# Placing global keys and queries a batch ahead in short GpSimd copies, with the k and q casts moved into the attention

## The chip, the core and the metric

The kernel runs on one core of one Trainium2 chip. The metric is the device time of one execution in microseconds (us): it covers everything from the first to the last instruction and the little that lies around them. Before the change three runs took 376.73, 377.93 and 377.97 us, a median of 377.93 us.

The core's engines work side by side and only wait for one another through semaphores. PE is the matrix engine, ACT the activation engine, DVE the vector engine, POOL (GpSimd) the general engine, and SP an engine that here only issues DMAs. GpSimd issues DMAs as well, and it executes its list strictly in order: a copy that stands behind a DMA that has to wait, waits too.

## What is computed

Windowed attention with eight global positions, followed by a two-layer block with a sine activation. All inputs are float32.

```python
batch, n_heads, seq, head_dim = (8, 8, 576, 64)
window = 32
scores = scale * np.matmul(q, k.transpose(0, 1, 3, 2))
mask = np.abs(pos[:, None] - pos[None, :]) <= window
mask = mask | is_global[:, None] | is_global[None, :]
scores = np.where(mask, scores, -1000000000.0)
attn = softmax(scores)
x = np.matmul(attn, v)          # heads side by side: 4608 tokens x 512
h = x @ w_in                    # 512 -> 2048
s = np.sin(alpha * h)
g = h + s * s / (alpha + 1e-09)
out = g @ w_out                 # 2048 -> 512
```

(The softmax is written out in the reference; the eight entries of `global_idx` mark the global positions.)

## The kernel before

The work goes batch by batch, b = 0 to 7. For each batch there is an attention (`phase_a`, `attention`) over four pairs of heads, and then a GEMM with w_in (`gemm1`) over sixteen groups of 128 hidden units. The second GEMM, with w_out (L1041), is cut into single matmuls that `fill` drops between the other work, so that PE has something to do. The kernel's order is written out by hand; each engine takes its own instructions in the order in which the program names them.

**Operands of the attention.** A batch's keys lie in `KX` and its queries in `QX`, two buffers each, taken in turn by `b % 2`. `KX` has, for each pair of heads and each of twelve tiles of 48 tokens, 128 columns; 8 of every 64 are the global keys. `QX` has four columns for global queries in each of seven places of a row. The values lie in `VX`, likewise with two buffers.

**How a batch's operands arrive.**
- `cast_qk(b)` (L324, DMAs at L329): GpSimd issues two DMAs of 576 KB each, k first and then q, which turn float32 into bf16 in a DRAM buffer of the pool `dramp` (two buffers for each of the two).
- `turn_qk(b)` (L334, L338): SP issues two transposing DMAs from there into the tiles `kt` and `qt`.
- `place(b, ...)` (L343, copies at L348 and L355): DVE copies from `kt` and `qt` into `KX` and `QX`. From batch 3 on the eight copies for batch b are spread over the attention of batch b - 1; two of them come at its very end (`beside(NHP)`, L880). For batch 3, in the attention of batch 2, four of them do.
- `place_globals(b)` (L365): GpSimd copies the global keys from `kTg` (two copies of 64 partitions by 384 elements, L369) and the global queries from `qTg` (two of 128 by 112, L374) into the other columns of `KX` and `QX`.
- `load_v(b, hps)` (L386, DMAs at L391): GpSimd issues four DMAs for each pair of heads. They overwrite the buffer that batch b - 2 used, so each group of four waits until PE has finished that pair's products (L781). `load_vg(b)` (L396) does the same for the global values from SP. A DMA of GpSimd's also waits for the landing of the DMA eight places earlier in its list, whose semaphore it shares.

**Inside an attention,** for each pair of heads: scores on PE (L739), exp on ACT (L747), the mask on DVE (L750), the two products with the values and with ones on PE (L781), the inverse of the sums on ACT (L807, L810), sums for the global positions (L791) and the normalising product (L813) on DVE. The products of the next pair of heads need the PSUM bank that L813 reads. Beside this, DVE squares the previous batch's x for a later check (L915, L920, L923). After the last pair come the reciprocal and two small products for the global rows (L823, L827).

**Inside gemm1,** for each group of 128 hidden units: eight matmuls on PE (L982), sine on ACT (L1014), its square on ACT (L1018) or DVE (L1020), and the sum into `H2` on DVE (L1022), which frees the PSUM bank. Three banks go round, so the fourth group waits for the first group's L1022.

**The main loop** decides the order on GpSimd. For batches 1 to 5 it issues, ahead of `gemm1(b)`, the casts for batch b + 2, the first pair's V loads, the placing for batch b + 1, and then the other V loads. For batch 0 the placing of batch 1 stands inside `gemm1`, for batch 6 that of batch 7 stands alone:

```python
        if 0 < b and b + 2 < B:
            cast_qk(b + 2)
            load_v(b + 2, (0,))

            place_globals(b + 1)
            load_v(b + 2, range(1, NHP))
            load_vg(b + 2)
        elif 0 < b < B - 1:
            place_globals(b + 1)
        gemm1(b)
```

The attention of batch b stands in the program before iteration b, and GpSimd runs ahead until the V loads make it wait for that attention's products. So the placing for batch b + 1 is executed in the midst of the attention of batch b.

Of the kernel before, what the change touches and what calls it, by code (L numbers as in the profile page):

```python
# [18 lines left out]
NG = 8  # L19
KT = 48  # L20
# [227 lines left out]
def kernel(  # L248
# [11 lines left out]
    nc = tc.nc  # L260
    B, H, S, D = q.shape
# [3 lines left out]
    NT12 = S // KT  # L265
    NHP = H // 2
# [27 lines left out]
    KX = [main.tile([P, NHP, NT12, P], DT.bfloat16, name=f"KX{i}") for i in range(2)]  # L294
# [9 lines left out]
    kTg = main.tile([P, NHP, NG, B], DT.bfloat16, name="kTg")  # L304
# [19 lines left out]
    def cast_qk(b):  # L324

        cast[b] = []
        for src, name in ((k, "kd"), (q, "qd")):
            t = dramp.tile([P, H * S * D // P], DT.bfloat16, name=name)
            nc.gpsimd.dma_start(  # L329
                out=t[:], in_=src[b].rearrange("h s d -> (h s d)").rearrange("(p f) -> p f", p=P)  # L330
            )
            cast[b].insert(0, t)

    def turn_qk(b):  # L334

        turned[b] = [trp.tile([P, H * HALF], DT.bfloat16, name=name) for name in ("qt", "kt")]
        for i in (1, 0):
            nc.sync.dma_start_transpose(  # L338
                out=turned[b][i][:], in_=cast[b][i][:].rearrange("p (r c) -> (p r) c", c=P)
            )  # L340
        del cast[b]
# [22 lines left out]

    def place_globals(b):  # L365

        for t in range(2):
            rows = slice(t * D, (t + 1) * D)
            nc.gpsimd.tensor_copy(  # L369
                out=KX[b % 2][rows, :, :, t * D + KT : t * D + KT + NG],  # L370
                in_=kTg[rows, :, None, :, b].to_broadcast([D, NHP, NT12, NG]),
            )
        for y in range(2):
            nc.gpsimd.tensor_copy(  # L374
                out=globals_of(b, slice(0, P), y),
                in_=qTg[:, :, None, y::2, b].to_broadcast([P, NHP, 7, 4]),
            )

    def globals_of(b, rows, y):

        q0 = QX[b % 2][rows, :, y, PAD : PAD + 4]
        return bass.AP(
            tensor=q0.tensor, offset=q0.offset, ap=[list(q0.ap[0]), [2 * QROW, NHP], [SEG, 7], [1, 4]]
        )

    def load_v(b, hps=range(NHP)):  # L386
        for hp in hps:
            for t in range(2):
                for y in range(2):
                    r = t * D + y * 24  # L390
                    nc.gpsimd.dma_start(  # L391
                        out=VX[b % 2][r : r + 24, hp, :, t * D : t * D + D],
                        in_=v[b, 2 * hp + t].rearrange("(i a y) d -> y a i d", a=24, y=2)[y],
                    )

    def load_vg(b):  # L396
        for h in range(H):
            t = h % 2
            src = VGb[b::B, h * D : (h + 1) * D] if b else VG0[h::H]
            nc.sync.dma_start(  # L400
                out=VX[b % 2][t * D + KT : t * D + KT + NG, h // 2, :, t * D : t * D + D],
                in_=src[:, None, :].to_broadcast([NG, NT12, D]),
            )
# [35 lines left out]
    for half in range(2):  # L439
        for w, src in ((1, k), (0, q)):  # L440
            nc.gpsimd.dma_start(
                out=nat[w][D * half : D * half + HK],
                in_=src[0, HH * half : HH * half + HH].rearrange("h (i r) d -> (h i) (r d)", r=KT),
# [22 lines left out]
    for t in (gidx8, gp64):  # L466
        nc.vector.memset(t[:].bitcast(DT.int32), 0)
    nc.sync.dma_start(
        out=g64[:],
        in_=bass.AP(tensor=global_idx.tensor, offset=global_idx.offset, ap=[[1, NG], [0, B], [1, 1]]),  # L470
# [3 lines left out]
    for t in (0, D):  # L474
        nc.sync.dma_start(out=gp64[t + KT : t + KT + NG], in_=global_idx[:, None])
        nc.sync.dma_start(
            out=gidx8[t + KT : t + KT + NG],
            in_=bass.AP(tensor=global_idx.tensor, offset=global_idx.offset, ap=[[0, NG], [1, NG]]),
# [29 lines left out]
    for i, bits in enumerate((B - 1, D - 1)):  # L508
        nc.vector.tensor_scalar(
            out=rowi[:, i : i + 1], in0=prow[:], scalar1=bits, scalar2=None, op0=ALU.bitwise_and  # L510
# [6 lines left out]
        out=cond[:, 0:1], in0=pm, scalar1=float(NH), scalar2=float(1 - KT), op0=ALU.is_ge, op1=ALU.mult  # L517
# [3 lines left out]
        out=kpos[:], in0=pm, scalar=2.0, in1=cond[:, 0:1], op0=ALU.mult, op1=ALU.add  # L521
    )
    nc.vector.scalar_tensor_tensor(
        out=kpos[:], in0=cond[:, 1:2], scalar=float(4095 + KT), in1=kpos[:], op0=ALU.mult, op1=ALU.add
# [4 lines left out]
        out=rowf[0 : NG * B, 4:5], in0=rowf[0 : NG * B, 0:1], scalar=float(S), in1=rowf[0 : NG * B, 3:4], op0=ALU.mult, op1=ALU.add  # L529
# [19 lines left out]
    for name, src in (("k", k), ("q", q), ("v", v)):  # L549
        g0[name] = VG0 if name == "v" else setup.tile([NG * B, D], DT.bfloat16, name="g0" + name)  # L550
        nc.gpsimd.indirect_dma_start(
            out=g0[name][:], out_offset=None, in_=src[0].rearrange("h s d -> (h s) d"),
# [16 lines left out]
        out=band[:], in0=qrel[:], scalar1=float(WIN * WIN) + 0.5, scalar2=None, op0=ALU.is_le  # L569
    )  # L570
    for t in (0, D):
# [4 lines left out]
        out=M2, in_=band[:].rearrange("p e x c -> p e (x c)")[:, None].to_broadcast([P, 6, 2, WCOL])  # L576
# [49 lines left out]
    def place_global_queries(t, copy):  # L626
# [15 lines left out]
        out=first[:], in0=gf[:], scalar1=gpf[:, 0:1], scalar2=None, op0=ALU.not_equal  # L642
# [3 lines left out]
        out=later[:], in0=jrow[:], scalar1=pm, scalar2=float(-KT), op0=ALU.subtract, op1=ALU.is_ge  # L646
# [5 lines left out]
        out=cond[:, 2:3], in0=pm, scalar=float(KT + NG - 1), in1=cond[:, 1:2], op0=ALU.is_le, op1=ALU.mult  # L652
# [5 lines left out]
        out=far[:], in0=qpos[:], scalar1=float(WIN * WIN) + 0.5,  # L658
# [13 lines left out]
    for w, name in ((1, "k"), (0, "q")):  # L672
        pg[w] = both[0:D, 32 + w * 64 : 64 + w * 64].bitcast(DT.bfloat16)
        nc.tensor.transpose(
            out=pg[w][:], in_=g0[name][:], identity=identb[0 : NG * B, 0 : NG * B]
# [283 lines left out]
    def gemm1(b):  # L959
# [28 lines left out]
        for nt in range(NT):  # L988
# [9 lines left out]
            if b == 0 and nt == 11:  # L998

                load_w_out()  # L1000
                cast_globals_v()
                place_globals(1)
                load_v(1, (2, 3))
                load_vg(1)
# [94 lines left out]
    def phase_a(b_att, b_moe):  # L1099
        def beside(at):  # L1100

            if b_moe is None:
                if at == -1:
                    nc.vector.tensor_scalar(out=recipT[:], in0=alphaT[:], scalar1=1e-9, scalar2=None, op0=ALU.add)
                    nc.vector.reciprocal(out=recipT[:], in_=recipT[:])
                if at == 0:
                    second_half()
                    nc.gpsimd.memset(VX[1][:].bitcast(DT.int32), 0)
                    nc.gpsimd.memset(QX[1][:].bitcast(DT.int32), 0)
                    nc.gpsimd.memset(KX[1][:].bitcast(DT.int32), 0)  # L1110
                    turn_qk(1)
                    nc.gpsimd.tensor_copy(out=seen[:], in_=turned[1][1][0:1, 0:1])
                    load_w_in((2, 3))
                    load_v(1, (0, 1))
                    gather(v, gv)
                return
            if at == 0:
                if b_moe == 2:
                    column_norms(zn[:, 0, :])
                if b_moe >= 3:  # L1120
                    token_norms(b_moe - 3, zn[:, 1, :])
            if 0 <= at < 2 and b_moe:
                square_x(b_moe, at)
            if b_att == 1 and at == 0:
                place_rest(1)
                place_rest(0)
            for which, t, y in places_at(b_att, at):
                place(b_att + 1, which, t, y, nc.vector.tensor_copy)
            if b_moe == 0 and at == 2:
                turn_qk(2)  # L1130
            if b_moe == 1 and at in (2, 3):
                square_w(at)

        if b_moe is not None:
            waiting.append(gemm2(b_moe))
        attention(b_att, beside)

    phase_a(0, None)
    for b in range(B):
        if 0 < b and b + 2 < B:  # L1140
            cast_qk(b + 2)
            load_v(b + 2, (0,))

            place_globals(b + 1)
            load_v(b + 2, range(1, NHP))
            load_vg(b + 2)
        elif 0 < b < B - 1:
            place_globals(b + 1)
        gemm1(b)
        if b + 1 < B:  # L1150
            if b == 0:
                cast_qk(2)
                load_v(2)
                load_vg(2)
            elif b + 2 < B:
                turn_qk(b + 2)
            phase_a(b + 1, b)
# [45 lines left out]
```

## Time and profile before

| what | value |
|---|---|
| median of three runs | 377.93 us (376.73 to 377.97) |
| the profiled execution | 376.68 us, of which its span is 375.0 us |
| mean granted PE clock | 0.991 |
| first scores of batches 2, 3, 4, 5, 6, 7 | 97.99, 140.69, 181.25, 221.32, 261.59, 300.78 us |
| GpSimd's copies L369 | 14, mean 1018 ns; shortest 862 ns |
| GpSimd's copies L374 | 14, mean 463 ns; shortest 371 ns |
| DVE's L1022, 576 wide | 805 to 817 ns |
| casts, from issue to landing (median) | k 6.4 us, q 8.9 us |

The profile is that of one execution. Times on the left of a timeline are microseconds from the start of the span, followed by the length, the engine, the line of the program, the operation and its tiles; `x4` joins four equal instructions that follow one another. In square brackets stands the time that the engine was idle before, and what ended it. Two operations in a row are read with care: a record can begin while the one before it is still finishing, so it is the length beside a like instruction elsewhere that tells of a delay.

### The profile page before, as it was taken

The page shows a single profiled execution, that of the slowest core. Times are in us where ns is not written, and L with a number is a line of the kernel's source. Part 1 is how long each engine was busy: PE and PEld are TensorE (multiplying, and loading weights), DVE is VectorE, ACT ScalarE, POOL GpSimd, SP SyncE. Part 2 cuts the span into 40 slices and gives each one's busy share as a digit, 9 for nine tenths or more (in the row PEclk, how much of TensorE's full clock was granted, in tenths as well). Part 3 has the DMA queues.
Part 4 walks back from the last instruction along what each step waited for, and adds up shares of the span by engine and source line. Part 5 has one row for each costly group of instructions (what it writes and reads, how often), then busy time and mean ns, then how long its engine had stood idle before and what let it go on. Part 6 is the DMA issues. An engine that isn't in the chain of part 4 may idle for free. (4 is left out here: it accounts for less than half of the span.)

```text
span 375.0 us, 8335 instructions
## 1 busy us (share of the span) xinstructions
PE 337.6 (90%) x2994; PEld 228.9 (61%) x3040; DVE 287.8 (77%) x624; ACT 294.1 (78%) x566; POOL 132.1 (35%) x204
## 2 busy tenths in 40 slices
PE   1578979998998899999989999999999999999992
PEld 1467646765566666667657766667676766665441
DVE  5776997589789887988888888888788876789400
ACT  7789997899889788788978897879888788875110
POOL 7993695578277001840087005740000000000001
PEclk9999999999999999999999999999999999999998
DMA  7999999999988863799159934636221001000221
GB/s 118 115 174 192 152 166 179 160 208 163 207 164 75 138 110 78 91 104 216 31 60 105 187 69 69 64 52 111 74 50 38 0 30 59 29 2 28 75 68 49
DMA packets 103578, 38.06 MB, mean 102 GB/s; under 512 B 94138, under 2 KB 98250, under 8 KB 103082
## 3 DMA queue, kind: packets, MB, share of 16 engines
q0 software_dynamic: 56640, 18.56, 42.7%
q1 hardware_dynamic: 46890, 18.89, 23.9%
q8 instruction: 26, 0.43, 0.5%
q14 instruction: 22, 0.18, 0.1%
HBM read 37.15 MB, written 17.83 MB: 147 GB/s over the span
## 5 line engine op out<-in xcount | busy, mean ns | idle before, releaser
L1041 PE MATMUL zo<-w_out,H 128*128 128x512 bf16 x530 | 143.3, 379 | 1.9
L982 PEld LDWEIGHTS <-w_in 128*128 128x128 bf16 x1024 | 98.6, 98 | 48.0 <-issue 12.6
L391 POOL DMA_DIRECT2D VX<-in_v_dram x128 | 83.1, 658 | 106.8 <-PE zd L781 90.4
L1041 PEld LDWEIGHTS <-H 128*128 128x128 bf16 x576 | 52.2, 97 | 37.9 <-issue 0.3
L747 ACT ACTIVATE E<-ring 128x480 bf16<-128x480 f32 x96 | 54.3, 568 | 25.5 <-PE ring L739 24.8
L750 DVE TENSOR_TENSOR E<-E,MASK 128x480 bf16<-128x480 bf16 x96 | 36.5, 410 | 16.7 <-ACT E L747 15.6
L1022 DVE SCALAR_TENSOR_TENSOR H<-s,recipT,zn 128x576 bf16<-128x576 bf16 x47 | 38.2, 814 | 8.4 <-ACT s L1018 5.0
L1018 ACT ACTIVATE s<-sb 128x576 bf16<-128x576 bf16 (+1 forms) x62 | 42.7, 689 | 2.0
L1069 POOL DMA_INDIRECT out_dram<-osb,grow x1 | 1.0, 1003 | 122.6 <-SPq L1171 122.6
L739 PE MATMUL ring<-QX,KX 128*128 128x120 bf16 x384 | 38.2, 226 | 6.5 <-ACT E L747 3.0
L739 PEld LDWEIGHTS <-KX 128*128 128x128 bf16 x384 | 29.1, 102 | 22.6 <-issue 11.0
L1014 ACT ACTIVATE sb<-zn,alphaT 128x576 bf16<-128x576 f32 (+1 forms) x47 | 34.8, 740 | 9.7 <-PE zn L982 9.7
L1022 DVE SCALAR_TENSOR_TENSOR H<-s,recipT,zd 128x576 bf16<-128x576 bf16 x39 | 31.7, 814 | 6.6 <-ACT s L1018 4.7
L1020 DVE TENSOR_TENSOR s<-sb 128x576 bf16<-128x576 bf16 (+1 forms) x66 | 31.1, 472 | 5.7 <-ACT sb L1014 5.4
L1047 ACT COPY osb<-zo 128x512 f32<-128x512 f32 x36 | 20.8, 578 | 18.4 <-PE zo L1041 18.4
L1022 DVE SCALAR_TENSOR_TENSOR H<-s,recipT,zr 128x576 bf16<-128x576 bf16 x39 | 31.7, 812 | 3.9 <-ACT s L1018 1.9
L1014 ACT ACTIVATE sb<-zd,alphaT 128x576 bf16<-128x576 f32 (+1 forms) x39 | 28.9, 741 | 6.9 <-PE zd L982 5.4
L781 PEld LDWEIGHTS <-VX 128*128 128x128 bf16 x448 | 26.0, 98 | 12.5 <-issue 6.8
L1014 ACT ACTIVATE sb<-zr,alphaT 128x576 bf16<-128x576 f32 (+1 forms) x39 | 28.9, 741 | 4.4 <-PE zr L982 4.4
L982 PE MATMUL zn<-xlast,w_in 128*128 128x288 bf16 (+1 forms) x192 | 28.8, 289 | 1.2 <-DVE H L1022 0.7
L781 PE MATMUL zn<-E,VX 128*128 128x120 bf16 (+2 forms) x336 | 26.3, 209 | 3.7 <-DVE xlast L813 2.2
L982 PE MATMUL zn<-xT,w_in 128*128 128x288 bf16 x184 | 26.9, 286 | 3.0 <-DVE H L1022 1.9
(161 smaller groups left out, 489.8 us busy)
## 6 DMA issues: line engine op xcount, KB each, us to landing
VX<-in_v_dram POOLq DMA_DIRECT2D x128, 36.0 KB, 3.9
kd<-in_k_dram POOLq DMA_DIRECT2D x7, 576.0 KB, 6.4
qd<-in_q_dram POOLq DMA_DIRECT2D x7, 576.0 KB, 8.9
w_in<-in_moe_w_in_dram POOLq DMA_DIRECT2D x4, 512.0 KB, 5.7
w_out<-in_moe_w_out_dram POOLq DMA_DIRECT2D x4, 512.0 KB, 8.9
out_dram<-osb SPq DMA_DIRECT2D x8, 256.0 KB
out_dram<-osb SPq DMA_DIRECT2D x8, 224.0 KB
out_dram<-osb SPq DMA_DIRECT2D x8, 192.0 KB
```

Of the source, the lines that this page charges most:

```text
L391: nc.gpsimd.dma_start(out=VX[b % 2][r : r + 24, hp, :, t * D : t * D + D], in_=v[b, 2 * hp + t].rearrange("(i a y) d -> y a i d", a=24, y= ...
L739: nc.tensor.matmul(out=ps[:, e * WCOL : (e + 1) * WCOL], lhsT=kx[:, hp, i, :], rhs=qx[:, hp, :, s0 : s0 + 60], start=True, stop=True, skip ...
L747: nc.scalar.activation(out=Eg, in_=ps[:, 0 : 4 * WCOL], func=AF.Exp, scale=scale, accum_out=EA[:, n : n + 1])
L750: nc.vector.tensor_tensor(out=Eg, in0=Eg, in1=MASK[:, 4 * g : 4 * g + 4, :].rearrange("p i c -> p (i c)"), op=ALU.mult,)
L781: nc.tensor.matmul(out=out_t[:, half, :, a - half * CUT : z - half * CUT], lhsT=OB[:] if key else VXb[:, hp, i, :], rhs=E[:, i, :, a - s0 ...
L982: nc.tensor.matmul(out=h[e][:, 0:W], lhsT=lhsT, rhs=xT[:, c, e, 0:W], start=(c == 0), stop=(c == CT - 1), skip_group_check=True,)
L1014: nc.scalar.activation(out=sb[:, es, 0:W], in_=h[:, :, 0:W], func=AF.Sin, scale=alphaT[:, nt : nt + 1])
L1018: nc.scalar.activation(out=s2[:, :, 0:W], in_=sb[:, :, 0:W], func=AF.Square)
L1020: nc.vector.tensor_tensor(out=s2[:, :, 0:W], in0=sb[:, :, 0:W], in1=sb[:, :, 0:W], op=ALU.mult)
L1022: nc.vector.scalar_tensor_tensor(out=H2[:, nt, r0 : r0 + S].rearrange("p (e c) -> p e c", e=2)[:, es], in0=s2[:, es, 0:HALF], scalar=recip ...
L1041: nc.tensor.matmul(out=ops[:], lhsT=H2[:, nt, blk * P : (blk + 1) * P], rhs=w_out[:, nt, :], start=(nt == 0), stop=(nt == NT - 1),)
L1047: nc.scalar.copy(out=osb[:], in_=ops[:])
```

## The change

`place_globals` copies the global keys for one pair of heads at a time: eight copies of 64 by 96 elements in place of two of 64 by 384. The two copies of the queries stay.

In the main loop the placing for batch b + 2 is issued in iteration b, behind the V loads of the first three pairs of heads; before, it was that of b + 1, behind the first pair's. Iteration 1 keeps the placing of batch 2 where it was and adds that of batch 3. Iteration 6 places nothing any more. The casts for batches 5, 6 and 7 are issued in iterations 2, 3 and 4, between the V loads of the first and the second pair; before, they opened iterations 3, 4 and 5. The casts for batches 3 and 4 stay at the head of iterations 1 and 2.

```diff
     def place_globals(b):
 
-        for t in range(2):
-            rows = slice(t * D, (t + 1) * D)
-            nc.gpsimd.tensor_copy(
-                out=KX[b % 2][rows, :, :, t * D + KT : t * D + KT + NG],
-                in_=kTg[rows, :, None, :, b].to_broadcast([D, NHP, NT12, NG]),
-            )
+        for hp in range(NHP):
+            for t in range(2):
+                rows = slice(t * D, (t + 1) * D)
+                nc.gpsimd.tensor_copy(
+                    out=KX[b % 2][rows, hp, :, t * D + KT : t * D + KT + NG],
+                    in_=kTg[rows, hp, None, :, b].to_broadcast([D, NT12, NG]),
+                )
...
         if 0 < b and b + 2 < B:
-            cast_qk(b + 2)
+            if b < 3:
+                cast_qk(b + 2)
             load_v(b + 2, (0,))
-
-            place_globals(b + 1)
-            load_v(b + 2, range(1, NHP))
+            if b == 1:
+                place_globals(2)
+            elif b + 3 < B:
+                cast_qk(b + 3)
+            load_v(b + 2, (1, 2))
+            place_globals(b + 2)
+            load_v(b + 2, (3,))
             load_vg(b + 2)
-        elif 0 < b < B - 1:
-            place_globals(b + 1)
         gemm1(b)
```

In the built program PE, DVE, ACT and SP have the same instructions in the same order as before, each waiting for the same engines; only GpSimd's list differs. The lines after `place_globals` move down by one.

## The prediction, made before the changed kernel had run

> **What bounds the kernel now.** I read the busy shares first, then PE's waits in order of time, then DVE and GpSimd at the same moments. The chain that ended last covers under 1% of the span (it is the tail's last scatter), so it is no guide here.
>
> ```profile
> PE 337.6 (90%) x2994; PEld 228.9 (61%) x3040; DVE 287.8 (77%) x624; ACT 294.1 (78%) x566; POOL 132.1 (35%) x204
> ```
>
> PE sets the time, so only a moment in which PE stands idle can be won. In the attentions of batches 3, 4 and 5 there is exactly one such moment each. PE's timeline:
>
> ```profile
> 156.16 0.36 PE L781 MATMUL zn<-E,VX 128*128 128x88 bf16 x4 [0.84 <-DVE xlast L813]
> ...
> 196.63 0.36 PE L781 MATMUL zn<-E,VX 128*128 128x88 bf16 x4 [1.03 <-DVE xT L813]
> ...
> 236.76 0.36 PE L781 MATMUL zn<-E,VX 128*128 128x88 bf16 x4 [0.84 <-DVE xlast L813]
> ```
>
> PE waits 0.84, 1.03 and 0.84 us for the normalising product L813. DVE at that place in batch 4 (with copies of GpSimd beside it) and in batch 6 (without any):
>
> ```profile
> 191.04 1.95 DVE L920 TENSOR_TENSOR SQ<-SQ 128x1152 bf16<-128x1152 bf16 x2
> 193.03 0.89 DVE L923 TENSOR_TENSOR SR<-SQ 128x288 bf16<-128x288 bf16 x1
> 193.93 0.57 DVE L355 COPY KX<-kt 64x1152 bf16<-64x1152 bf16 x1
> 194.54 1.11 DVE L750 TENSOR_TENSOR E<-E,MASK 128x480 bf16<-128x480 bf16 x3
> ```
>
> ```profile
> 271.37 1.24 DVE L920 TENSOR_TENSOR SQ<-SQ 128x1152 bf16<-128x1152 bf16 x2
> 272.65 0.31 DVE L923 TENSOR_TENSOR SR<-SQ 128x288 bf16<-128x288 bf16 x1
> 272.97 0.45 DVE L355 COPY KX<-kt 64x1152 bf16<-64x1152 bf16 x1
> 273.46 1.05 DVE L750 TENSOR_TENSOR E<-E,MASK 128x480 bf16<-128x480 bf16 x3
> ```
>
> The same work is 0.71 + 0.58 + 0.12 + 0.06 = 1.47 us longer in batch 4. GpSimd then:
>
> ```profile
> 191.31 2.44 POOL L369 COPY KX<-kTg 64x384 bf16<-64x384 bf16 x2
> 193.81 0.93 POOL L374 COPY QX<-qTg 128x112 bf16<-128x112 bf16 x2
> 194.69 2.60 POOL L391 DMA_DIRECT2D VX<-in_v_dram  x4
> 198.35 2.54 POOL L391 DMA_DIRECT2D VX<-in_v_dram  x4 [1.07 <-PE zd L781]
> ```
>
> So these four copies of place_globals and DVE's bf16 work hold each other up; in batch 6, where the kernel places nothing, PE has no such gap. L1022, with one operand in PSUM, keeps 807 to 817 ns in all 125 of its 576-wide runs, copies beside it or not: it is not touched.
>
> **What the removal is worth.** Measure from the first scores of an attention to the fourth w_in group of the GEMM behind it: 140.69 to 165.08 = 24.39 us in batch 3, 24.16 in batch 4, 24.36 in batch 5, and 23.27 (261.59 to 284.86) in batch 6. From there to the next first scores it is 15.91 in batches 4 and 5 and 15.92 in batch 6, so the difference is kept: 1.12 + 0.89 + 1.09 = 3.10 us for the three. The lower bound is the three gaps alone less the 0.25 us that batch 6 waits at its fourth group, 2.71 - 0.75 = 1.96. In batch 2 placing (107.92 to 111.09) also ran beside DVE, but there ACT runs without a pause from 109.05 to 119.8 and sets the end of the attention: gain 0.
>
> **Where the copies go.** PE, DVE, ACT and SP keep their streams, and the engines they wait for. GpSimd alone is reordered: for batches 4 to 7 the placing now stands behind the third of four groups of V loads, which waits for the products of head pair 2, so it falls on the end of the attention. The eight KX copies have 96 elements. Alone a 384-element copy takes 0.87 us and a 112-element one 0.37, so 1.8 ns per element and 0.34 us for 96; the placing grows from 1.77 + 0.69 = 2.5 to some 3.4 us. GpSimd is 35% busy and nobody waits for these columns until a whole batch later, so the length itself costs nothing.
>
> What is late next is DVE's chain into the GEMM, here in batch 6:
>
> ```profile
> 282.15 0.32 DVE L827 TENSOR_TENSOR xlast<-GS,RG 128x16 bf16<-128x16 f32 x2
> 282.48 0.92 DVE L348 COPY QX<-qt 64x1152 bf16<-64x1152 bf16 x2
> 283.43 0.46 DVE L1020 TENSOR_TENSOR s<-sb 128x576 bf16<-128x576 bf16 x1
> 284.00 0.81 DVE L1022 SCALAR_TENSOR_TENSOR H<-s,recipT,zn 128x576 bf16<-128x576 bf16 x1
> ```
>
> It ends at 284.81 and PE's fourth group starts at 284.86: no cover, every hit counts. In batch 6's frame L827 is at +20.56 and L1020 ends at +22.3. The third V group can start at +15.9, but its fourth DMA must wait for the DMA eight places earlier. That wait is seen once today, behind casts:
>
> ```profile
> 67.94 0.64 POOL L391 DMA_DIRECT2D VX<-in_v_dram  x1 [1.01 <-DMA kd<-in_k_dram]
> 70.83 0.64 POOL L391 DMA_DIRECT2D VX<-in_v_dram  x1 [2.26 <-DMA qd<-in_q_dram]
> ```
>
> In the new order the cast of q stands eight places before it. It would be issued at +10.6 (V loads from +7.44, 2.63 us, then 0.53 for k) and takes 8.9 to land (the page's median), +19.5; behind that DMA stand the ten copies and the last V group; the copies run from about +20.1 to +23.5. They meet L827 twice, L348 twice and L1020: 5 hits in batches 3 and 4. In batch 5 no cast stands there, copies run from +18.5, four pieces are left by +20.56: 4 hits. In batch 2 L348 has four copies (121.06, 1.99 us); pieces are left for 5 hits. Together 19.
>
> Price of a hit: the 112-element copies cost L355 0.12 (0.57 against 0.45), L750 0.06 to 0.07 (three times) and 0.2 (twice, 110.25: 1.43 for three), L1020 0.18 (0.63 against 0.45): mean 0.125, a third of 0.37. A 384-element copy costs 0.39 (L1020, 0.84) to 0.58 (L923), about 0.52 of its 0.87. So 0.25 to 0.35 of a copy is hidden, and a piece of 0.34 costs 0 to 0.09; I take 0.05, the cut of the same instruction being the nearest row. Eight pieces at 0.05 and two at 0.125: 0.065 a hit, bounds 0.025 and 0.097. Cost 19 x 0.065 = 1.24 (0.5 to 1.8).
>
> **The early batches.** place_globals(3) moves into the GEMM of batch 1, 92 to 95.5: five hits of 0.065 on L355 and L348 there, 0.33, of which about 0.2 is cover (PE's last group starts at 95.93, its L1022 ends at 95.69): 0.13, up to 0.3. The shorter pieces of place_globals(2) replace L1020's 0.84 and 0.63 in front of PE's gap of 0.59 at 85.75: -0.3 (0 to -0.4). place_globals(1) likewise shortens L348's pair of 1.25 at 50.44: -0.2 (0 to -0.4).
>
> **The casts.** They fly in the attention, not under the GEMM. Issuing costs GpSimd 0.53 each, as before. V loads queued behind them land some 9 us later, for use 30 us on. Cast 6 today overlaps the transposes of batch 5 (5.37 us to issue at 169.11, against 2.67 at 134.56); that ends, and nobody waited. Outputs on SP share the engines with the casts; no PE or ACT wait in these stages names a DMA, and the three osb buffers cover it. I count 0; without that cover ACT's L1047 would be late.
>
> **Sum.** -3.10 + 1.24 + 0.13 - 0.3 - 0.2 = -2.2 us. The profiled execution took 376.68 (span 375.0 and 1.7 around it), so 374.5; its time lies 1.25 under the median of 377.93, where the same step gives 375.7, my forecast. With all bounds together: -3.4 (-3.10 + 0.5 + 0 - 0.4 - 0.4) to +0.2 (-1.96 + 1.84 + 0.3).
>
> **Rivals.** (1) *The hits cost as much as they did.* One price decides: with h per hit the sum is -3.6 + 19h + (5h - 0.2), level at 0.16. At 0.125, as the 112-element rows, it is -0.8: 377.1, no change to be told. For it: eight of ten pieces are almost that length. Against: the proportion above.
>
> (2) *Slower: each operation waits out a whole piece.* At h = 0.34 the sum is -3.8 + 24 x 0.34 = +4.4: 382.3. Place: L827 to L1020 behind each attention. For it: L923's 0.58 was more than half of a long copy, and a queue of ten pieces always has one ready. Against: no row shows a whole copy lost. The Trainium skill, "SBUF — State Buffer", section "SBUF: two separate sides", says this of the port pair that GpSimd shares with VectorE: whichever starts first holds it "for the whole instruction" and the other blocks fully. By that rule splitting a copy does not divide the lock, it deals it out to more operations, and rival 2 follows; the rows agree that L1022 is spared and that an operation blocks, but a hit of 0.12 beside a copy of 0.37 is less than the whole.
>
> (3) *Casts land early*, the third V group isn't held, and the copies end beside L813: two hits each, 8 x 0.065 = 0.5, the sum -3.4: 374.5.
>
> That the change misses its aim, because PE's gaps have another cause, is refuted well by batch 6; I give it no case.
>
> **How the numbers follow.** Forecast 0.60, rival 1 0.14, rival 2 0.16, rival 3 0.10. Half a per cent, about what a measurement of this kernel tells from no change, is 1.9 us. Of the forecast's 0.60 I put 0.42 beyond it and 0.18 within. Faster 0.42 + 0.10 = 0.52, same 0.18 + 0.14 = 0.32, slower 0.16. The forecast's own range is 374.5 to 378.1 on the median; since the profiled execution lies lower I start at 373.6, and reach to 379.0 towards rival 2.
>
> **What would show it.** PE's waits for L813 at the second product of batches 3 to 5 gone, L920 and L923 there back at 1.24 and 0.31; GpSimd's copies beside L827 to L1020, L348's pair at 1.0 to 1.1 and L1020 at 0.5; PE's fourth group waiting 0.3 to 0.6 for L1022; first scores to fourth group at 23.5 to 23.7. Wrong if L1020 or L348 grow by 0.3 each, if the placing takes over 5 us, or if PE or ACT waits for a DMA.

## The result and the profile after

The changed kernel takes 373.98 us (median of 12 executions, 372.53 to 376.25) beside 377.34 us for the kernel before on the same chip (12 executions, 376.09 to 380.35). The ratio is 0.9911, with a 95% interval of 0.9884 to 0.9938: 3.4 us faster. A second measurement of the same kernel, with other runs beside it, gave 373.06 us and 0.990 (0.9872 to 0.9929). Ratios leave disturbed executions out, so for a kernel whose executions scatter the median and the ratio need not agree.

The profiled execution took 373.89 us, its span is 372.2 us. In code behind `place_globals` the line numbers are one higher than before: L813 is now L814, L1022 is L1023. The busy shares come first:

```profile
PE 336.6 (90%) x2994; PEld 228.8 (61%) x3040; DVE 282.8 (76%) x624; ACT 293.5 (79%) x566; POOL 140.2 (38%) x246
```

DVE is 5.0 us less busy with the same 624 instructions, and GpSimd 8.1 us more with 42 more. PE's timeline at the second product of batches 3, 4 and 5, where it stood 0.84, 1.03 and 0.84 us for L813:

```profile
156.10 0.36 PE L782 MATMUL zn<-E,VX 128*128 128x88 bf16 x4
...
195.36 0.36 PE L782 MATMUL zn<-E,VX 128*128 128x88 bf16 x4
...
234.69 0.36 PE L782 MATMUL zn<-E,VX 128*128 128x88 bf16 x4
```

No bracket stands behind them: the three gaps are gone. DVE just ahead of that place in batch 4:

```profile
190.97 1.24 DVE L921 TENSOR_TENSOR SQ<-SQ 128x1152 bf16<-128x1152 bf16 x2
192.24 0.31 DVE L924 TENSOR_TENSOR SR<-SQ 128x288 bf16<-128x288 bf16 x1
192.56 0.45 DVE L355 COPY KX<-kt 64x1152 bf16<-64x1152 bf16 x1
193.05 1.04 DVE L751 TENSOR_TENSOR E<-E,MASK 128x480 bf16<-128x480 bf16 x3
```

All four are back at the lengths that batch 6 had before. GpSimd's timeline in the same batch shows where the copies went, and what held them:

```profile
200.71 0.64 POOL L392 DMA_DIRECT2D VX<-in_v_dram  x1 [1.71 <-DMA qd<-in_q_dram]
201.34 3.49 POOL L370 COPY KX<-kTg 64x96 bf16<-64x96 bf16 x8
204.89 0.98 POOL L375 COPY QX<-qTg 128x112 bf16<-128x112 bf16 x2
```

And DVE beside them, with PE's fourth w_in group behind:

```profile
201.41 0.47 DVE L828 TENSOR_TENSOR xlast<-GS,RG 128x16 bf16<-128x16 f32 x2
201.90 1.04 DVE L348 COPY QX<-qt 64x1152 bf16<-64x1152 bf16 x2
202.97 0.49 DVE L1021 TENSOR_TENSOR s<-sb 128x576 bf16<-128x576 bf16 x1
203.56 0.81 DVE L1023 SCALAR_TENSOR_TENSOR H<-s,recipT,zn 128x576 bf16<-128x576 bf16 x1
```

```profile
203.18 1.03 PE L1042 MATMUL zo<-w_out,H 128*128 128x512 bf16 x4
204.43 1.14 PE L983 MATMUL zn<-xT,w_in 128*128 128x288 bf16 x8 [0.23 <-DVE H L1023]
```

PE runs five matmuls of w_out there; the first has no record in this profile, only its weight load has. Against the same instructions in batch 6 of before (0.32, 0.92, 0.46) the new collisions lengthen DVE's chain by 0.15 + 0.12 + 0.03 = 0.30 us, and PE now stands 0.23 us for the last of it.

The profiled span is 2.77 us shorter (374.96 to 372.19), and the stages say where: the first scores of batch 0 come 0.36 earlier; batches 0 and 1 together take 1.06 more; the stage of batch 2 (first scores to fourth w_in group) takes 0.25 more; those of batches 3, 4 and 5 take 1.01, 0.91 and 1.01 less; what follows the fourth group of batch 7 takes 0.59 less; the rest, a few hundredths at a time, makes 0.20.

### The profile page after: what moved, and what is told of

Its sections match the earlier page's. It is cut to its first block, busy times and chain, and to the rows that moved or that the text cites. A ratio compares the mean times of both kernels' runs of the same rounds, so it can differ in the third digit from the quotient of the medians.

```text
span 372.2 us, 8377 instructions
## 1 busy us (share of the span) xinstructions
PE 336.6 (90%) x2994; PEld 228.8 (61%) x3040; DVE 282.8 (76%) x624; ACT 293.5 (79%) x566; POOL 140.2 (38%) x246
## 5 line engine op out<-in xcount | busy, mean ns | idle before, releaser
L1023 DVE SCALAR_TENSOR_TENSOR H<-s,recipT,zn 128x576 bf16<-128x576 bf16 x47 | 38.2, 814 | 9.0 <-ACT s L1019 5.6
L1023 DVE SCALAR_TENSOR_TENSOR H<-s,recipT,zd 128x576 bf16<-128x576 bf16 x39 | 31.7, 814 | 6.5 <-ACT s L1019 4.6
L1021 DVE TENSOR_TENSOR s<-sb 128x576 bf16<-128x576 bf16 (+1 forms) x66 | 30.5, 463 | 6.2 <-ACT sb L1015 5.9
L1048 ACT COPY osb<-zo 128x512 f32<-128x512 f32 x36 | 20.8, 576 | 18.3 <-PE zo L1042 18.2
L1023 DVE SCALAR_TENSOR_TENSOR H<-s,recipT,zr 128x576 bf16<-128x576 bf16 x39 | 31.7, 813 | 4.2 <-ACT s L1019 2.1
```

Source lines behind the costliest of these rows:

```text
L1021: nc.vector.tensor_tensor(out=s2[:, :, 0:W], in0=sb[:, :, 0:W], in1=sb[:, :, 0:W], op=ALU.mult)
L1023: nc.vector.scalar_tensor_tensor(out=H2[:, nt, r0 : r0 + S].rearrange("p (e c) -> p e c", e=2)[:, es], in0=s2[:, es, 0:HALF], scalar=recip ...
L1048: nc.scalar.copy(out=osb[:], in_=ops[:])
```

## The experiments

Every kernel was run beside the kernel before. The stages are those of the one profiled execution, in us; medians and ratios are over all executions of that measurement.

| kernel | batch 2 | batch 3 | batch 4 | batch 5 | median us (before) | ratio (95%) |
|---|---|---|---|---|---|---|
| before | 26.52 | 24.39 | 24.16 | 24.36 | 377.34 | 1 |
| after | 26.77 | 23.38 | 23.25 | 23.35 | 373.98 (377.34) | 0.9911 (0.9884–0.9938) |
| after, again | 26.61 | 23.47 | 23.25 | 23.36 | 373.06 (376.41) | 0.990 (0.9872–0.9929) |
| nothing placed from batch 3 on | 26.46 | 23.38 | 22.97 | 23.35 | 373.24 (376.41) | 0.9916 (0.9895–0.9937) |
| before, short copies | 29.25 | 23.62 | 23.19 | 23.59 | 373.82 (376.08) | 0.9941 (0.992–0.9962) |
| before, placed later | 26.93 | 23.33 | 23.06 | 23.55 | 376.05 (376.08) | 0.9966 (0.9934–0.9999) |
| before, casts moved | 27.33 | 24.88 | 24.64 | 24.35 | 378.45 (376.08) | 1.0072 (1.0046–1.0099) |
| after, long copies | 27.91 | 24.88 | 24.82 | 23.35 | 385.56 (376.08) | none |
| after, casts back | 26.63 | 23.39 | 23.14 | 30.08 | 380.76 (376.41) | 1.0105 (1.0031–1.018) |
| the same, batch 1 long | 26.63 | 23.37 | 23.11 | 30.27 | 380.49 (376.41) | 1.013 (1.0076–1.0184) |
| casts back, all transposes sooner | 39.03 | 23.39 | 23.11 | 23.38 | 385.49 (376.57) | 1.0216 (1.0187–1.0245) |
| placed later, all transposes sooner | 39.61 | 23.34 | 23.06 | 23.35 | 387.29 (376.57) | 1.0243 (1.0187–1.0298) |
| casts back, one transpose pair sooner | 26.63 | 23.37 | 23.10 | 23.36 | 373.71 (376.38) | 0.9929 (0.9904–0.9954) |
| after, batch 1 long | 26.59 | 23.53 | 23.18 | 23.39 | 373.51 (376.57) | 0.9914 (0.9894–0.9934) |

### What the copies cost: none placed, and the kernel after again

```diff
             load_v(b + 2, (0,))
-            place_globals(b + 1)
+            if b == 1:
+                place_globals(2)
             load_v(b + 2, range(1, NHP))
             load_vg(b + 2)
-        elif 0 < b < B - 1:
-            place_globals(b + 1)
```

> The kernel before without the placing for batches 3 to 7 (their global keys and queries stay those of batches 1 and 2, so that part of the attention is left out of the computation); batches 1 and 2 are placed as before, casts as before. It is the bound for any place and length of the copies. Theory P: stages of batches 3 to 5 at 23.27 as batch 6, time 2.5 to 4 us below before; after is within 0.7 us of it, that is, the new collisions cost next to nothing. Rival (a cause other than the copies holds L813 up in batches 3 to 5): stages 24 and more.

> The kernel after once more, so that the next three stand beside it on one chip. Stages 23.4, 23.25 and 23.35 in batches 3 to 5 as in its first profile. Time 2 to 4 us below before. First scores of batch 1 at 53.7 if the w_in load lands early in this execution (PE's wait for it 0.2 us), at 54.9 if late (1.9).

Without any placing the stages of batches 3 to 5 lose 1.01 + 1.19 + 1.01 = 3.21 us, and the time is 0.9916 of before. So the copies are the cause, and the kernel after (0.9911 and 0.990) stands at this bound. Batch 4 falls below the 23.27 that theory P named: with no copies at all PE has no wait at its fourth group,

```profile
202.22 1.24 PE L1041 MATMUL zo<-w_out,H 128*128 128x512 bf16 x5
203.41 1.14 PE L982 MATMUL zn<-xT,w_in 128*128 128x288 bf16 x8
```

where batch 6 of before waits 0.25. Against this bound the new collisions of the kernel after cost 0.00, 0.28 and 0.00 us in batches 3, 4 and 5, and 0.09, 0.28 and 0.01 in its second run. The other theory (stages of 24 and more) is out. The second run of after gave its stages again; its first scores of batch 1 came at 54.31, with 1.3 us of waiting for w_in, between the two cases that were named.

### One part of the change at a time

Short copies in the old place and order (the change to `place_globals` alone):

> The kernel before, with the eight short copies at the old places and nothing moved. Stage = first scores to fourth w_in group, 24.39, 24.16 and 24.36 us in batches 3, 4 and 5 before, 23.38, 23.25 and 23.35 after. Theory P (the shared work of DVE and GpSimd: the gain is that the placing no longer lies in front of L813): the ten pieces still stand there, at 0.03 to 0.13 a hit for some six hits, 0.2 to 0.8 of the 1.47 us of DVE delay is left, so PE's gap mostly closes too: stages 23.4 to 23.9, time 1 to 2.5 us below before. Rival L (only the length of the pieces matters, the place doesn't): stages as after, 23.3. Rival C (the casts' flight is what was in the way): stages unchanged at 24.2 to 24.4, time as before. In the start of batch 1 the longer placing makes PE's wait for its first scores longer by up to 1.4 us by all of them.

Long copies, placed behind the third V group, casts as before (the main loop's change without the casts):

> The kernel before, with only the place of the placing moved: behind the third pair's V loads and a batch ahead, in the two long copies; casts at their old place. Theory P: DVE in front of L813 is free, L920 and L923 at 1.24 and 0.31; with no cast in its way the third group of V loads isn't held, so the copies start at +18.5 of the stage and end by +21; one long copy can still meet L827 or L348 (0.5) and the query copies L348 (0.12 each): stages 23.3 to 23.9, time 1.5 to 3 us below before. Rival L: a long copy costs the same 1.47 wherever it lies, stages 24 or more and time as before. Rival C: time as before.

The casts alone (long copies in the old place):

```diff
         if 0 < b and b + 2 < B:
-            cast_qk(b + 2)
+            if b < 3:
+                cast_qk(b + 2)
             load_v(b + 2, (0,))
+            if b > 1 and b + 3 < B:
+                cast_qk(b + 3)
             place_globals(b + 1)
```

> The kernel before, with only the casts moved (those of batches 5 to 7 behind the first pair's V loads of iterations 2 to 4). Theory P: the placing comes 1.1 us later and stays in the attention; DVE's delay moves from L920 to the operations 1 us later (L923, L355, L750), the PE gaps stay within 0.3 of 0.84 to 1.03, time within 0.7 us of before. Rival C: stages at 23.3, time 2 to 3.5 us below before.

The kernel after with the two long copies put back into `place_globals`:

> The kernel after, with the two long copies back. Theory P: in batches 3 and 4 the copies are held by the cast of q until about +20, so two long copies meet L827, L348 and L1020 at 0.4 to 0.58 each for two or three hits and the query copies at 0.12: stages 24.0 to 24.6, no gain there; in batch 5 no cast stands in the way and the stage is 23.4 to 23.8. PE's wait at the start of batch 1 is shorter than after by 0.5 to 1.4. Time 0.5 to 2.5 us above after. Rival (the length makes no difference at the new place): stages as after, time 0 to 1.4 us below after.

The three stages of before sum to 72.91 us. Short copies alone take 2.51 off, the later place alone 2.97, both with the casts (the kernel after) 2.93. In these three stages either half does nearly the whole work: short pieces leave PE no wait for L813 even in the old place, and long ones hardly do harm behind the third V group. The stages of the later place are those that its theory P named; those of the short copies are too in batches 3 and 5, while batch 4 came as low as in the kernel after. By time the two halves reach 0.9941 and 0.9966, beside 0.9911 for the whole change, with intervals that overlap. The casts alone make it slower, by 0.7%. Their two DMAs stand ahead of the long copies, which then start about a microsecond later and cover the second L920 and L923 whole; GpSimd and DVE of that kernel in batch 4:

```profile
194.78 1.96 POOL L369 COPY KX<-kTg 64x384 bf16<-64x384 bf16 x2
```

```profile
193.55 2.45 DVE L920 TENSOR_TENSOR SQ<-SQ 128x1152 bf16<-128x1152 bf16 x2
196.03 0.87 DVE L923 TENSOR_TENSOR SR<-SQ 128x288 bf16<-128x288 bf16 x1
```

2.45 where the kernel before had 1.95. That is 0.8 us in batch 2 and 0.5 in batches 3 and 4, and nothing in batch 5, where no cast stands there. Theory P had the mechanism but allowed PE's gaps only 0.3 and the time 0.7 us; the gaps grew by up to 0.65 and the time by 2.4. A gain from the casts as such is out.

Long copies with the casts moved show what the short ones are needed for. GpSimd and DVE of that kernel, again batch 4:

```profile
203.60 0.64 POOL L391 DMA_DIRECT2D VX<-in_v_dram  x1 [2.18 <-DMA qd<-in_q_dram]
204.24 1.79 POOL L369 COPY KX<-kTg 64x384 bf16<-64x384 bf16 x2
```

```profile
203.82 1.48 DVE L827 TENSOR_TENSOR xlast<-GS,RG 128x16 bf16<-128x16 f32 x2
205.31 1.59 DVE L348 COPY QX<-qt 64x1152 bf16<-64x1152 bf16 x2
206.93 0.52 DVE L1020 TENSOR_TENSOR s<-sb 128x576 bf16<-128x576 bf16 x1
```

The q cast, eight places earlier, holds the V load and so the copies until they fall on L827: 1.16 + 0.67 + 0.06 us longer, and the stages are 24.88 and 24.82. In batch 5 no cast holds them, and the stage is 23.35. The pattern is that of theory P; the sizes lie a little outside it (24.0 to 24.6 and 23.4 to 23.8). Half of this kernel's four executions took 393 and 397 us, so it has no ratio; these two were not profiled and their cause is open.

Two things did not fit. The later place with long copies was as fast as the kernel after in its profiled execution (373.07 us), yet four of its ten executions took 380 to 385. And short copies alone had one bad stage, batch 2 with 29.25, in a profiled execution of 377.27 us where most others took 373 to 374. GpSimd and ACT of that execution:

```profile
98.20 0.54 POOL L329 DMA_DIRECT2D kd<-in_k_dram  x1
100.60 0.53 POOL L329 DMA_DIRECT2D qd<-in_q_dram  x1 [1.87 <-DMA VX<-in_v_dram]
```

```profile
118.89 0.59 ACT L1048 COPY osb<-zo 128x512 f32<-128x512 f32 x1 [2.50 <-DMA out_dram<-osb]
```

These casts landed at 115.0 and 117.3 us, 17 us after their issue and not 6 to 9, and ACT stood for an output store that was in flight with them.

### What the casts' move is for

The kernel after with the casts of batches 5 to 7 back at the head of iterations 3 to 5:

```diff
         if 0 < b and b + 2 < B:
-            if b < 3:
-                cast_qk(b + 2)
+            cast_qk(b + 2)
             load_v(b + 2, (0,))
             if b == 1:
                 place_globals(2)
-            elif b + 3 < B:
-                cast_qk(b + 3)
             load_v(b + 2, (1, 2))
```

> The kernel after with the casts of batches 5 to 7 back at the head of iterations 3 to 5. No cast then stands eight places before the third group of V loads, so the copies start at +18.5 and not +20.1 of the stage. Theory P (the casts' move wins nothing, it only delays the copies onto L348 and L1020): stages 23.1 to 23.5, all three like batch 5; batch 2 shorter by 0 to 1; time 0 to 2 us below after. Rival C2 (the casts' earlier flight wins something, by taking them off the transposes): time 0.7 to 2.5 us above after, with a wait for kt or qt, or a longer one for an output store, in the profile.

Batches 3 and 4 came as theory P said, 23.39 and 23.14. But the stage of batch 5 took 30.08 us and the whole 380.76, so theory P fell. Rival C2 had the sign and the wait for kt, though it put the loss at 0.7 to 2.5 us above after, and it was 7. DVE and PE in batch 5:

```profile
227.61 0.92 DVE L355 COPY KX<-kt 64x1152 bf16<-64x1152 bf16 x2 [5.57 <-DMA kt<-kd]
```

```profile
230.10 0.53 PE L782 MATMUL zn<-E,VX 128*128 128x88 bf16 x4 [4.20 <-DVE low L933]
```

The cause lies 20 us earlier, on SP and GpSimd:

```profile
205.05 3.52 SPq L338 DMA_TRANSPOSE kt<-kd  x1
208.68 19.03 SPq L338 DMA_TRANSPOSE qt<-qd  x1
```

```profile
206.05 0.54 POOL L329 DMA_DIRECT2D kd<-in_k_dram  x1
206.57 0.54 POOL L329 DMA_DIRECT2D qd<-in_q_dram  x1
```

GpSimd runs a batch ahead: these are the transposes of batch 6 and the casts of batch 7. The casts were issued 1.0 us behind the first transpose and landed 19.4 and 21.1 us later; SP needed 19.03 us to issue the second transpose. The DMA engines from 206 to 228 us of this kernel (busy tenths, and GB/s):

```profile
DMA  9999999919090190399009093099190991903959
GB/s 141 110 148 144 145 222 236 69 34 5 0 50 0 34 5 0 56 54 40 0 0 51 0 39 1 0 341 237 0 472 0 265 202 34 441 0 67 160 21 269
```

From the ninth slice to the twenty-sixth, some 10 us, nothing is above 56 GB/s, now with the engines busy, now with none. Then PE's stop has a price of its own. By windows of this kernel (PE, PEld, DVE, ACT and POOL busy, granted clock, DMA share, GB/s):

```profile
230.00:240.00 10.00, 9.90 (x97) 7.05 (x97) 6.85 (x18) 5.55 (x15) 4.26 (x7) 0.73 0.35 42
```

With a granted clock of 0.73 for 10 us, an estimated 2.7 us (10 x 0.27) are added to the 4.2 of standing: 6.9 in all, against the 30.08 - 23.35 = 6.7 that the stage lost. The same kernel with the first placing in long copies lost it again in the same place (30.27, casts 1.0 us behind the transpose).

Theory D says that it is the meeting of the two, the casts coming shortly behind the transposes. To part them, the transposes go ahead of the VG loads on SP:

```diff
             load_v(b + 2, (3,))
+            turn_qk(b + 2)
             load_vg(b + 2)
...
-            elif b + 2 < B:
-                turn_qk(b + 2)
```

> e5 with one thing moved: the two transposes of a batch stand ahead of the eight VG loads on SP, so they should be issued at about +15 of the stage (196 in batch 4) instead of +24 (205), and be through before the casts at 206. Theory D (in e5 the casts, issued 1.0 us behind the start of the transposes, bring the DMA engines to a standstill): the standstill goes, the wait of L355 for kt (5.6 us) with it, the stage of batch 5 is 23.1 to 23.6, and the time is 371 to 374. Rival (the short copies and late casts cost the 7 us in another way, or casts behind V loads are slow by themselves): stage of batch 5 at 27 to 30 again, time 378 and more. A second collision that would also speak for D: transposes that now meet the V loads of 189 to 206 and take 5 to 10 us.

> e2 (placing sooner, in long copies, casts as before) with the transposes ahead of the VG loads. e2 had casts 0.4 us ahead of the transposes, and 4 of its 10 executions took 380 to 385 us, the others 373 to 377. Theory D (those four are the same standstill, which comes or not by a few tenths of a microsecond in that order): no execution above 377, median 372 to 374.5. Rival (those four have another cause): again a spread of 8 us and more. Stages of batches 3 to 5 at 23.1 to 23.6 by both.

The stage of batch 5 went to 23.38 and 23.35, as theory D has it, but the time went up to 385.49 and 387.29: a wait that no theory named. ACT's waits in the first of the two:

```profile
ACT osb L1048 <- DMA out_dram<-osb: 12.3, 1, 12.3
```

In batch 2 SP stood at the transposes, which there wait for the last of DVE's copies out of the tiles kt and qt, and the output stores that ACT's L1048 needs stood behind them. The times therefore say nothing of theory D, and the second kernel nothing of the scatter it was made for. So, last, only the pair that meets the casts is moved:

```diff
             load_v(b + 2, (3,))
+            if b == 4:
+                turn_qk(6)
             load_vg(b + 2)
...
-            elif b + 2 < B:
+            elif b + 2 < B and b != 4:
                 turn_qk(b + 2)
```

> e5 with the two transposes of batch 6 alone ahead of the VG loads, those of the other batches where e5 has them. e10 moved them all, and in batch 2 ACT's L1048 then stood 12.3 us for an output store queued behind them on SP; the stage of batch 5 was 23.38 there, against 30.08 in e5. Theory D (the whole loss of e5 is the meeting of batch 6's transposes with batch 7's casts): transposes at about +15 of batch 4's stage, no wait of L355 for kt, stage of batch 5 at 23.1 to 23.6, no long wait for osb, time 371 to 374, level with after. Rival (another cost of late casts and short copies remains): 376 and more.

SP's, GpSimd's and DVE's rows, and the DMA engines from 206 to 228 us:

```profile
195.70 2.18 SPq L338 DMA_TRANSPOSE kt<-kd  x1
202.09 2.18 SPq L338 DMA_TRANSPOSE qt<-qd  x1
```

```profile
205.65 0.54 POOL L329 DMA_DIRECT2D kd<-in_k_dram  x1
```

```profile
221.57 0.91 DVE L355 COPY KX<-kt 64x1152 bf16<-64x1152 bf16 x2
```

```profile
DMA  9990393983970568200000000010002930004700
GB/s 135 143 582 0 67 402 67 304 169 68 403 135 11 131 138 221 96 7 0 0 0 0 0 0 0 0 30 0 0 0 74 279 123 0 0 0 197 279 0 0
```

The casts are where they were, within half a microsecond, and land in 5.8 and 8.4 us. L355 waits for nothing, the stage is 23.36 and the time 373.71 us, 0.9929 of before and level with after. Only the position of two transposes, ahead of eight VG loads instead of behind them, differs from a kernel that takes 380.76. That their meeting with the casts cost the 7 us is shown; why the engines come near a standstill in it is not.

When it comes is known only in part, and the distance between the issues does not settle it. In the profiled executions casts issued 2.5 and 4.5 us ahead of the transposes (before), and 0.4 ahead (placed later), landed in 6 to 10 us; 0.9 to 1.0 us behind the start of a transpose they took 17 to 22 us in three kernels (casts back, the same with batch 1 long, and short copies in batch 2). But 0.9 to 1.0 us behind the start of the second transpose of batch 3 they landed in 7 to 10 us in two others (placed later, and after with long copies).

The packets in the traces tell these cases apart. A transpose moves 2304 packets of 256 bytes. In the three bad meetings 1454 to 1539 of them had started when the first packet of the casts did, 3.4 to 4.7 us after the cast's issue, so the casts came into the midst of a transpose. In every other meeting of a profiled execution, those two included, the transpose at hand had at most 89 packets left or had not begun. The scatter of the placed-later kernel could have the same cause, but none of its long executions was profiled.

### The placing of batch 1

Short copies for all batches but the first, on the kernel with the casts back and on the kernel after:

```diff
-        for hp in range(NHP):
+        if b == 1:
+            for t in range(2):
+                rows = slice(t * D, (t + 1) * D)
+                nc.gpsimd.tensor_copy(
+                    out=KX[b % 2][rows, :, :, t * D + KT : t * D + KT + NG],
+                    in_=kTg[rows, :, None, :, b].to_broadcast([D, NHP, NT12, NG]),
+                )
+        for hp in range(NHP if b > 1 else 0):
```

> As e5, and the placing of batch 1 in the two long copies. In after PE waits 2.0 us for the last query copy of that placing before the first scores of batch 1; before it waited 1.8 for DVE's L348. Theory S (ten short copies take 3.9 us there instead of 2.5, and the scores wait for them): the wait names DVE again, first scores 0.3 to 1.4 us earlier at the same landing of w_in, time 0.3 to 1.4 us below e5. Rival (that wait only follows the late landing of w_in): first scores as in e5 at the same landing, time within 0.3 of it.

> The kernel after with the placing of batch 1 in the two long copies, the rest as after. Theory S (ten short copies take 3.9 us there instead of 2.5 and hold the first scores of batch 1): the wait for L375's QX is gone, the first scores of batch 1 are 0.3 to 1.0 us earlier at the same landing of w_in, time 0.3 to 1.0 us below after (0.987 to 0.989 of before, where after had 0.990 and 0.991). Rival: within 0.3 us of after, the wait then names DVE's L348 with the same length.

PE's waits before batch 2, in the kernel after and then in after with batch 1 long:

```profile
PE ring L740 <- POOL QX L375: 2.0, 1, 2.0
PE zn L983 <- DMA w_in<-in_moe_w_in_dram: 1.9, 1, 1.9
```

```profile
PE ring L747 <- DVE QX L348: 1.8, 1, 1.8
...
PE zn L990 <- DMA w_in<-in_moe_w_in_dram: 0.7, 1, 0.7
```

The name of the wait changes, the time doesn't: 0.9914 (0.9894 to 0.9934), as after. From the first scores of batch 0 to those of batch 2 it is 82.35 us with the long copies, 82.92 and 82.25 in the two profiles of after. The other kernels with long first copies lie at 81.39 to 83.49, the others with short ones at 82.17 to 82.55. PE's wait for w_in differs between executions too, from none to 1.9 us, but does not order these times: without one the placed-later kernel takes 82.55, and with 0.8 us of it the shortest takes 81.39. What moves this stretch by 2 us stays open. Theory S is not borne out, and an effect under half a microsecond would not be seen.

## Why the prediction was right, point by point

- *PE's gaps come from copies and DVE holding each other up, worth 3.10 us in batches 3 to 5.* Right, cause and size: with nothing placed the stages lose 3.21 us. No wait of either names the other; it is the operations themselves that grow longer, which the opening's sentence on engines and semaphores leaves out. The lengths given for L1022 start at 805 ns, not 807; that changes nothing. Nothing to gain in batch 2: right, 26.46 against 26.52.
- *The copies stand behind the q cast in batches 3 and 4, not in batch 5.* Right: GpSimd waits 1.93 and 1.71 us for it, and the copies start at +20.7, +20.2 and +18.7 of their stages, against the forecast of +20.1 and +18.5. Rival 3 needed them early and is out.
- *The placing grows to 3.4 us.* Mis-sized: 4.2 to 4.5 us in the new place. A short copy alone does take the 0.34 to 0.36, but they start 0.4 us apart even undisturbed (eight in 3.13 us in batch 1), and they are themselves held up by DVE.
- *A hit costs 0.065 us.* Right on DVE in batch 4, 0.30 us over five operations, 0.06 each; 0.16 over five in batch 3 and 0.14 over four in batch 5 are 0.03 each, near the lower bound. Rivals 1 (0.125) and 2 (0.34) are out. The Trainium skill, "SBUF — State Buffer", section "SBUF: two separate sides", on which rival 2 leaned, has the port pair held "for the whole instruction"; here an operation that meets a 0.34 us copy loses 0.03 to 0.06.
- *"No cover, every hit counts": 1.24 us for 19 hits.* This is the step that failed. Measured against the kernel that places nothing, the hits cost PE 0.00 + 0.28 + 0.00 us in batches 3, 4 and 5 and 0.31 in batch 2, together 0.59 (0.53 in the second run of after), and the stages came at 23.25 to 23.38 instead of 23.5 to 23.7. Batch 6 was taken as the frame for all, but GpSimd does nothing there; in batch 3 it issues V loads when it places nothing, and DVE's second L348 takes 0.62 us beside them instead of 0.46:

```profile
161.72 1.09 DVE L348 COPY QX<-qt 64x1152 bf16<-64x1152 bf16 x2
```

With the copies the pair takes 1.05, and L1023 ends 23.33 us after the first scores in both kernels: the hits take the place of another delay. In batch 5 DVE's L1020 stood 0.20 us for ACT when nothing is placed, and the longer L348 fills that. In batch 4 nothing absorbs them. So in these three batches the hits cost DVE 0.60 us where 14 x 0.065 = 0.91 was forecast, and PE 0.28 of it.

- *The early batches: -0.37 in all.* The gap of 0.59 in batch 1's GEMM did shrink to 0.20, as forecast, while the next one grew from 0.63 to 0.77. The sum did not show: batches 0 and 1 took 1.06 us more in one profile and 0.38 in the other, where like kernels differ by 2 us. The term was too small to be seen beside that.
- *The casts: 0.* Right for this change: the first transpose is issued in 3.0 and 2.7 us instead of 5.4 and 7.5, and no wait of PE or ACT in these stages names a DMA. But the reasoning was short: it asked what the casts' move removes and not what the later placing does to the casts when they stay. They are pushed behind the copies, from 2.5 us ahead of the transposes to 1.0 behind, and that costs 7 us. Against the kernel before the move alone costs 0.7%; beside the short copies in the new place it is what keeps the gain.
- *Sum -2.2 us.* The profiles differ by 2.79 and the medians by 3.36. The median of 373.98 is within the range, but only 0.4 us above its lower end and below the 374.5 that all bounds together gave. The collisions account for 0.65 of the difference; the remaining half microsecond is within the interval of the measurement. By its number rival 3 (374.5) came nearest, by luck: its copies were not early, and with the forecast's other terms its sum is -3.10 + 0.52 + 0.13 - 0.3 - 0.2 = -2.95 and not -3.4. The shorter tail (0.59) and the earlier start (0.36) in the profiled execution are no terms of the change that any run here could confirm.

## What to carry to other kernels

Ask of each part of a change not only what it wins alone: here the casts alone cost 0.7% and the short copies with the later placing but without the casts' move cost 1%, while all three together win 0.9%. When a queue is reordered, write down for every DMA on it which other DMAs it now meets, and at which point of their transfer: casts that came ahead of a transpose were harmless here, and the same casts in the midst of one made PE stand. A kernel that leaves the suspected work out costs one run and gives the bound, and it corrects the frame of reference stage by stage.

## What the runs showed of the hardware

- A GpSimd copy's price for DVE is far from proportional to its length: at the same place behind batch 4 the placing in short copies lengthened L828 to L1021 by 0.30 us, 0.06 per meeting with a copy of 0.34, and the placing in long copies L827 to L1020 by 1.89. By these figures some 0.28 us of each short copy cost DVE nothing, so cutting the copies to 0.34 us took away five sixths of the delay.
- Casts that came into the midst of a transpose came near a standstill with it: 576 KB took 17 to 22 us instead of 6 to 10, with 10 us below 60 GB/s. In the kernel with the casts back 115 of the transposes' 4608 packets of 256 bytes took 1.0 to 4.1 us, most of them about 1.4 or 2.75, where the median is 0.02; a cast's packet of 18 KB took 1.38. From 209.5 to 220 us only eight of the casts' 64 packets started, and behind most of them, within 0.4 us, ten to twenty of those long ones. The Trainium skill, "DMA: Bandwidth & Descriptors", section "Queues, rings and completion order", has each DMA engine alternate between queues packet by packet, so a transpose's packet may well stand behind a cast's, as the lengths of 1.4 and 2.75 suggest; that does not explain the stretches in which nothing moves.
- After PE had stood for 4.2 us its granted clock was 0.50 for 5 us and 0.96 for the next 5, 0.73 in all, which by the estimate above made the loss over half as large again.
